# Filling four fifths instead of 0.55 of TensorE's planned gaps, in a kernel of windowed attention and a two-layer network

## The chip, the cores and the metric

The kernel runs on one core of one Trainium2 chip. The metric is the device time of one execution in microseconds (us), and where several executions were timed their median is given. The core has a matrix engine (TensorE, "PE" in the profile, with its weight loads on a row "PEld" of their own), a vector engine (VectorE, "DVE"), a scalar engine (ScalarE, "ACT"), GpSimd ("POOL"), a queue engine that issues transfers (SyncE, "SP"), and 16 DMA engines.

## What is computed

Eight batches of eight heads, 576 positions, 64 numbers per head. Each position attends to its neighbours within 32 positions and to 8 global positions, and the global positions attend to all. The result, 4608 tokens of 512 numbers, goes through a two-layer network with a softplus between the layers.

```python
mask = np.abs(pos[:, None] - pos[None, :]) <= window      # window = 32
mask = mask | is_global[:, None] | is_global[None, :]
scores = np.where(mask, scale * q @ k.T, -1e9)
attn = softmax(scores); y = attn @ v                      # (8, 8, 576, 64)
x = y.transpose(0, 2, 1, 3).reshape(4608, 512)
out = softplus(x @ w_in) @ w_out                          # w_in 512 x 2048, w_out 2048 x 512
```

## The kernel before, in words

The work is cut into jobs, and each job is a short run of instructions on one engine. Per batch, q and k are loaded, rounded to bf16 and transposed. For the first two batches TensorE does the transposes (tile `tr`, lines 857 to 863); later ones are transposed by VectorE. Blocks of 32 positions are taken four at a time ("pairs", 36 in all). A pair's scores are made on TensorE (tile `s`, line 1077), go through subtraction of the maximum, exponential and normalisation on VectorE, ScalarE and GpSimd (tiles `m`, `st`, `rs`, `pn`), and are transposed on VectorE (`pt`). For the first four pairs the mask is added on TensorE by a product with the identity (lines 1060 and 1070), and the exponential is a row of small ScalarE instructions (line 1113). The rows and columns of the global positions have tiles of their own (`sg`, `pg`, `pgt`, `ov`, `vg`). Four pairs make a stage of 512 tokens: TensorE multiplies probabilities by values (`xo`, line 1251), the result is rounded (`xT`), and then come the first layer (`h`, line 1286, 128 x 512 results of four matmuls each), softplus on ScalarE (`g`, line 1292), the second layer (`o`, line 1297) and the copy and store of the output (`osb`). There are nine stages. The attention of the next stage is interleaved with the two layers of the present one.

The order is not left to the hardware. Class `_Order` is a planner that runs when the program is built. Every job has an estimated cost, dependencies, and the PSUM banks that it opens. A fixed list, `ORDER`, says which job is taken next and on which engine; the planner walks through the list, gives each job a planned time (in planned nanoseconds), chooses PSUM banks by which of the eight was planned to come free first, and then writes the instructions out in order of planned time. It also keeps an estimate of instruction fetch: `stall()` (line 45) counts TensorE's instructions in blocks of 256 (`BLOCK`), with a first need at instruction 448 (`NEED`) and a first request at 130 (`ASK`), and moves planned times where a block would be late. `self.issued` is that count.

Where the planner takes a job for TensorE, it calls `keep()` (line 155) with the planned end of TensorE's last job, t0, and the planned start of the next, t1. If the gap is at least 700 planned ns, lies before 34,000 planned ns (`WARM`, line 358), and a PSUM bank is free, `keep()` puts fillers into it. A filler is a 128 x 128 by 128 x 512 product of zeros into that bank whose result nobody reads (`fill_in`, line 725; tile `warm`, line 729 of the profile), two instructions each: a weight load and a matmul. Their number is the gap times a share over a planned 220 ns (line 166). With `NARROW` at 0 only `FILL` and `FILLT` of line 151 are in use. The fillers stand in TensorE's own queue, so a job behind them starts when they are done, even if its data came earlier. `keep()` then books the bank as used until the planned end of the fillers and adds two per filler to `self.issued`; it does not move `free["PE"]`.

In the kernel before, the planner meets seven such gaps, of 7750.8, 1012.8, 1072.8, 2053.0, 815.2, 2020.9 and 820.6 planned ns, and puts 19, 2, 2, 5, 2, 5 and 2 fillers into them.

Of the kernel before, what the change touches and what calls it, by code (L numbers as in the profile page):

```python
# [20 lines left out]
class _Order:  # L21
# [126 lines left out]
        return self.backs[x - 1][1] if x else 0  # L148

    WARM = 0  # L150
    FILL, FILLT, NARROW, NFILL, NFILLT = 0.55, 220, 0, 0.8, 140
    STARVE = 900
    fill = None

# [1320 lines left out]
```

## Time and profile before

| What | us |
|---|---|
| Median of three runs | 335.49 |
| Lowest and highest of them | 334.19, 336.04 |
| The profiled execution's own time | 333.06 |
| Its span, first to last instruction | 331.4 |
| TensorE busy within the span | 317.9 |
| ScalarE, VectorE, GpSimd busy | 231.7, 220.9, 193.3 |

The profile is of one execution. The span leaves out 1.66 us that lie around it in that execution's own time. A matmul's recorded duration contains the run through the array, so matmuls that follow each other overlap in the record; how often one starts is read from the starts, not from the durations. "Idle before, releaser" names what ended an engine's wait; "issue" there means that the engine waited for nothing that the profile shows.

### The profile page before, as it was taken

What the parts mean: (1) busy time and instruction counts of PE and PEld (TensorE: products, weight loads), DVE (VectorE), ACT (ScalarE), POOL (GpSimd) and SP (SyncE); (2) the same over time, 40 slices, a digit from 0 to 9 for tenths busy, and PEclk for the clock granted to TensorE, in tenths of its full rate; (3) what the DMA queues carried; (4) which work ended last, traced back from release to release, by engine and by line L of the source; (5) the groups of instructions that cost most, each with busy time, mean ns of one, the idle gap of its engine ahead of it and who ended that gap; (6) DMA issues with size and microseconds to landing.
All of it is one profiled execution on the core that took longest, in us unless ns stands there. A gap on an engine that the chain in (4) does not pass through costs nothing.

```text
span 331.4 us, 12080 instructions
## 1 busy us (share of the span) xinstructions
PE 317.9 (96%) x5281; PEld 168.8 (51%) x5281; DVE 220.9 (67%) x387; ACT 231.7 (70%) x460; POOL 193.3 (58%) x173
## 2 busy tenths in 40 slices
PE   8778998899999999999999999999999999999995
PEld 3537874576555444544454445445544454454453
DVE  7697578786995999993895498819966890440000
ACT  5799759696897678489778947866457467925712
POOL 7865654994783596878648675496327764420000
PEclk9999999999999999999999999999999999999999
DMA  7999899898878998996994759650001112000102
GB/s 192 185 201 223 166 201 177 139 184 187 154 122 156 169 209 157 203 227 112 157 188 75 179 135 143 150 168 3 4 0 65 36 65 95 2 34 32 65 16 112
DMA packets 168860, 42.14 MB, mean 127 GB/s; under 512 B 153320, under 2 KB 165864, under 8 KB 168808
## 3 DMA queue, kind: packets, MB, share of 16 engines
q1 hardware_dynamic: 155928, 27.15, 46.0%
q0 software_dynamic: 11008, 11.08, 17.0%
q10 hardware_dynamic: 1872, 3.15, 2.5%
q8 instruction: 41, 0.67, 0.9%
q14 instruction: 11, 0.09, 0.1%
HBM read 36.71 MB, written 9.44 MB: 139 GB/s over the span
## 4 chain that ended last, share of the span: by engine, by line
PE 71%; SPq 11%; DMA 9%; ACT 4%; issue 1%; POOL 1%; DVE 1%; POOLq 0%
PE o L1297 32%; PE h L1286 29%; SPq L464 5%; PE xo L1251 4%; DMA stage<-in_q_dram 4%; SPq L469 3%; PE s L1077 3%; DMA stage<-in_k_dram 3%; ACT st L1113 2%; DMA wout<-in_moe_w_out_dram 2%; PE ov L997 1%; DMA stage<-in_v_dram 1%; SPq L518 1%; PE pick L886 1%; SPq L514 1%
## 5 line engine op out<-in xcount | busy, mean ns | idle before, releaser
L1297 PE MATMUL o<-wout,g 128*128 128x512 bf16 (+1 forms) x592 | 138.6, 374 | 0.2 <-ACT g L1292 0.2
L1286 PE MATMUL h<-xT,win 128*128 128x512 bf16 (+3 forms) x768 | 136.7, 326 | 0.8 <-DMA win<-in_moe_w_in_dram 0.8
L1292 ACT ACTIVATE g<-h 128x512 bf16<-128x512 f32 (+3 forms) x192 | 83.9, 503 | 35.0 <-PE h L1286 33.4
L1286 PEld LDWEIGHTS <-win 128*128 128x128 bf16 x768 | 66.7, 98 | 59.7 <-issue 1.1
L1132 POOL TENSOR_TENSOR pn<-st,rs 128x1024 bf16<-128x1024 f32 (+1 forms) x36 | 64.7, 1806 | 42.9 <-DVE rs L1126 38.8
L1297 PEld LDWEIGHTS <-g 128*128 128x128 bf16 x592 | 55.5, 98 | 60.6 <-ACT g L1292 1.4
L1100 POOL TENSOR_TENSOR st<-st,m 128x1024 f32<-128x1024 f32 x32 | 60.5, 1899 | 28.3 <-DVE m L1094 28.2
L1124 DVE TENSOR_REDUCE sm<-st 128x8 f32<-128x1024 f32 x32 | 38.4, 1200 | 19.0 <-ACT st L1117 18.8
L1081 DVE TENSOR_TENSOR st<-s,mask 128x512 f32<-128x512 f32 x64 | 41.3, 678 | 9.3 <-PE s L1077 9.2
L1094 DVE TENSOR_REDUCE m<-st 128x8 f32<-128x1024 f32 x32 | 38.4, 1206 | 0.4
L1117 ACT ACTIVATE st<-st 128x1024 f32<-128x1024 f32 x32 | 32.7, 1051 | 3.2 <-POOL st L1100 3.0
L1141 DVE STREAM_TRANSPOSE pt<-pn 128x512 int32<-128x512 int32 x36 | 24.6, 693 | 10.4 <-POOL pn L1132 10.2
L720 ACT COPY osb<-o 128x512 f32<-128x512 f32 (+1 forms) x27 | 15.5, 575 | 20.3 <-PE o L1297 18.7
L720 ACT CAST xT<-xo 128x512 bf16<-128x512 f32 (+3 forms) x28 | 11.5, 474 | 14.5 <-PE xo L1251 14.5
L720 POOL CAST kb<-stage 128x1152 bf16<-128x1152 f32 (+2 forms) x9 | 11.5, 1273 | 10.8 <-DMA stage<-in_q_dram 8.8
L717 POOL TENSOR_SCALAR qb<-stage 128x1152 bf16<-128x1152 f32 (+1 forms) x11 | 12.9, 1177 | 8.1 <-DMA stage<-in_q_dram 6.5
L1292 ACT ACT_TABLE_LOAD x13 | 16.7, 1283 | 0.2
L1077 PE MATMUL s<-kx,qx 64*32 64x128 bf16 x1152 | 14.7, 220 | 1.3 <-issue 0.6
L720 DVE CAST xT<-xo 128x512 bf16<-128x512 f32 (+3 forms) x20 | 11.0, 582 | 6.5 <-PE xo L1251 6.5
L1077 PEld LDWEIGHTS <-qx 64*32 64x32 bf16 x1152 | 10.0, 90 | 10.3 <-issue 7.7
L720 POOL CAST vb<-stage 128x1152 bf16<-128x1152 f32 x9 | 10.3, 1150 | 6.8 <-DVE sm L1124 3.3
L1117 ACT ACT_TABLE_LOAD x11 | 14.1, 1283 | 0.2
(129 smaller groups left out, 301.6 us busy)
## 6 DMA issues: line engine op xcount, KB each, us to landing
stage<-in_v_dram SPq DMA_DIRECT2D x56, 144.0 KB, 4.2
stage<-in_k_dram SPq DMA_DIRECT2D x48, 144.0 KB, 4.1
stage<-in_q_dram SPq DMA_DIRECT2D x48, 144.0 KB, 3.5
out_dram<-osb POOLq DMA_DIRECT2D x24, 256.0 KB, 3.6
out_dram<-osb ACTq DMA_DIRECT2D x11, 256.0 KB, 2.0
stage<-in_q_dram SPq DMA_DIRECT2D x4, 512.0 KB, 6.5
stage<-in_k_dram SPq DMA_DIRECT2D x4, 512.0 KB, 7.4
wout<-in_moe_w_out_dram POOLq DMA_DIRECT2D x4, 512.0 KB, 7.8
```

Source lines behind the costliest of these rows:

```text
L720: {"ACT": nc.scalar.copy, "DVE": V.tensor_copy, "POOL": nc.gpsimd.tensor_copy}[e](out, in_)
L1077: nc.tensor.matmul(out=PS["s", n, g][quad(a), x, :], lhsT=qx[b % 2][rows(g), a, j * BL:(j + 1) * BL], rhs=kx[b % 2][rows(g), a, e0 * BL:(e ...
L1081: V.tensor_tensor(out=PS["st", n][:, h, :, :], in0=PS["s", n, h][:, :, :], in1=mask[:, h, j0:j0 + PB, :, :].rearrange("p j s i -> p j (s i ...
L1094: V.reduce_max(out=m[:], in_=flat(PS["st", n], h0, h1), axis=AX)
L1100: on(e).tensor_tensor(out=t, in0=t, in1=over(PS["m", n, y][:], SL * BL), op=OP.subtract)
L1117: nc.scalar.activation(out=t, in_=t, func=AF.Exp)
L1124: V.reduce_sum(out=sm[:], in_=flat(PS["st", n], h0, h1), axis=AX)
L1132: on(e).tensor_tensor(out=PS["pn", n][:, :, :, h0:h1].rearrange("p x s h -> p h x s"), in0=PS["st", n][:, h0:h1], in1=PS["rs", n, y][:].re ...
L1141: V.transpose(out=bass.AP(base.tensor, base.offset, ap=[list(base.ap[0]), [2 * STEP, PB // 2], [STEP + BL // 2, 2], [1, SL * BL]]), in_=PS ...
L1286: nc.tensor.matmul(out=h[:, :], lhsT=w_in_t[c // 4][:, kd, c % 4 * P:(c % 4 + 1) * P], rhs=PS["xT", m][:, kd, lo:hi], start=(kd == 0), sto ...
L1292: nc.scalar.activation(out=PS["g", m, c][:, lo:hi], in_=PS[key][:, lo_of(c, hi - lo)], func=AF.Softplus)
L1297: nc.tensor.matmul(out=PS["o", m, ns, a][:, :], lhsT=PS["g", m, kf][:, ns * P:(ns + 1) * P], rhs=w_out_t[kf // 4][:, kf % 4, a:z], start=( ...
```

## The change

One constant is raised, the share of each planned gap that is filled. The list `ORDER`, the lower limit of 700 planned ns, the planned 220 ns per filler and everything else are the same text.

```diff
     WARM = 0
-    FILL, FILLT, NARROW, NFILL, NFILLT = 0.55, 220, 0, 0.8, 140
+    FILL, FILLT, NARROW, NFILL, NFILLT = 0.8, 220, 0, 0.8, 140
     STARVE = 900
     fill = None
```

The line that uses it is `count = int((t1 - t0) * share / step)`, with `share, step` being `FILL, FILLT`.

## The prediction

> **What bounds the kernel now.** I read the page first, then who TensorE waited for, then the fillers, then TensorE's instructions in order of time, and last a count of its instructions.
>
> ```profile
> PE 317.9 (96%) x5281; PEld 168.8 (51%) x5281; DVE 220.9 (67%) x387; ACT 231.7 (70%) x460; POOL 193.3 (58%) x173
> PE   8778998899999999999999999999999999999995
> q8 instruction: 41, 0.67, 0.9%
> ```
>
> TensorE is busy for 96% of the span, and its only slices below nine tenths, but for the last, are the first eight or so: up to about 70 us it waits for others, after that it is the bound. An us that its queue loses after 70 us is an us at the end; one lost before can be swallowed by a later wait. The third line is a queue that brings 41 pieces of about 16 KB under the kind "instruction"; it matters below. Whom TensorE waited for (total, times, longest):
>
> ```profile
> PE sg L968 <- issue: 1.0, 1, 1.0
> ...
> PE h L1286 <- DMA win<-in_moe_w_in_dram: 0.8, 1, 0.8
> ...
> PE s L1077 <- issue: 0.6, 1, 0.6
> PE xo L1251 <- ACT osb L720: 0.4, 1, 0.4
> ...
> PE xo L1251 <- ACT g L1292: 0.4, 1, 0.4
> PE xo L1251 <- DVE pt L1141: 0.2, 1, 0.2
> PE s L1077 <- ACT kx L720: 0.2, 1, 0.2
> PE o L1297 <- ACT g L1292: 0.2, 1, 0.2
> ```
>
> Behind 70 us only the last row remains, 0.2 us: there is next to no slack to hide a loss in. Two waits, 0.6 and 1.0 us, are for "issue", for nothing that the profile shows.
>
> **How many fillers come.** The fillers of before, and where they stand:
>
> ```profile
> L729 PE MATMUL warm<-vb x37: 376/379/634, 1.3 to 26.4; 128*128 128x512 bf16 x37
> ```
> ```profile
> 1.26 6.67 PE L729 MATMUL warm<-vb 128*128 128x512 bf16 x19 [1.26 <-DVE vb L551]
> 8.01 0.40 PE L857 MATMUL tr<-ident,kb 128*128 128x128 bf16 x4
> ...
> 10.57 0.40 PE L857 MATMUL tr<-ident,kb 128*128 128x128 bf16 x4 [0.66 <-ACT kb L720]
> ...
> 15.11 0.31 PE L860 MATMUL tr<-ident,qb 64*64 64x64 bf16 x8 [0.89 <-DVE m L1092]
> ...
> 16.46 1.24 PE L729 MATMUL warm<-vb 128*128 128x512 bf16 x5
> 19.19 0.43 PE L968 MATMUL sg<-kx,qg 128*32 128x320 bf16 x8 [1.49 <-DVE qg L720]
> ```
>
> Groups of 2 stand ahead of the rows of 10.57 and 15.11, and three more, of 2, 5 and 2, follow up to 26.4 us, 37 in all. A gap with n fillers is 400n to 400(n+1) planned ns long (220 / 0.55 = 400), and now gets one per 275 (220 / 0.8). By the groups alone 19 become 27 to 29, each 2 becomes 2 to 4, each 5 becomes 7 or 8: 12 to 24 more in all. By the planner's gaps of the kernel before it is 28, 3, 3, 7, 2, 7, 2, that is 52, or 15 more. I take 15, and 30 more instructions, since each filler is a weight load and a matmul.
>
> **What they cost where they stand.** Five fillers take 1.24 us of which the last is 0.376, so one starts every (1.24 - 0.376) / 4 = 0.216 us. The first group grows by 9, 1.94 us. Its last filler frees the array at 1.26 + 6.67 - 0.16 = 7.77 (the 0.16 is 0.376 less 0.216), the transpose starts at 8.01, so 0.24 was spare and the first transposes come 1.7 us later. The second and third group add 0.22 each: 2.1 us of delay, against TensorE's waits of 0.66, 0.2 (`s` for `kx`) and 0.89 up to 15.11. Some 0.4 us is left if what ends those waits doesn't move. ScalarE must not move much for that:
>
> ```profile
> 9.38 1.14 ACT L720 CAST kb<-stage 128x512 bf16<-128x512 f32 x2 [0.90 <-DMA stage<-in_k_dram]
> 14.64 0.42 ACT L713 ACTIVATE qb<-stage 128x256 bf16<-128x256 f32 x1 [0.93 <-DMA stage<-in_q_dram]
> ```
>
> It waits there for transfers that TensorE has no part in, so a late copy of a transpose has 0.93 us of cover before 14.64. The fourth group's two more (0.43) lie in the 1.49 us before `sg`; the sixth's two (0.43) lie ahead of the 0.8 us before `h`. If these covers were gone, the whole 1.94 + 0.22 + 0.22 + 0.43 + 0.43 = 3.2 us would be the cost; what passes 28 us by this sum is 0 to 0.4, and the 1.0 us of waits of `xo` at 64 to 69 us (0.4, 0.4, 0.2 in the waits) can take it. I cost the fillers' time at nothing, with 1.1 us as the far end. A gain is excluded as far as the clock goes: PEclk is at nine tenths or more in every slice, and its longest wait behind the first filler is the 1.49 us before `sg`.
>
> **What they move.** Every instruction behind 26.4 us now stands 30 places later in TensorE's queue. TensorE's instructions before two times, matmuls and weight loads:
>
> ```profile
> 0.00:46.60 46.60, 39.59 (x860) 26.44 (x861) 35.26 (x92) 37.55 (x136) 30.52 (x62) 1.00 1.19 193
> 0.00:52.00 52.00, 44.24 (x988) 29.79 (x989) 39.61 (x98) 40.05 (x148) 34.59 (x65) 1.00 1.19 193
> ...
> 0.00:72.20 72.20, 62.53 (x1356) 40.60 (x1357) 55.83 (x127) 56.78 (x180) 51.22 (x76) 1.00 1.14 184
> ...
> 0.00:172.90 172.90, 163.03 (x3274) 92.79 (x3275) 139.57 (x259) 134.01 (x307) 120.09 (x123) 1.00 1.01 177
> ...
> 0.00:234.49 234.49, 224.62 (x4137) 122.52 (x4137) 182.02 (x330) 177.95 (x372) 161.80 (x153) 1.00 0.89 161
> 0.00:236.10 236.10, 226.23 (x4298) 124.04 (x4299) 183.56 (x332) 178.54 (x373) 162.29 (x154) 1.00 0.88 160
> 0.00:239.10 239.10, 229.23 (x4311) 125.41 (x4312) 186.53 (x336) 181.11 (x377) 163.70 (x154) 1.00 0.87 158
> ```
> ```profile
> 46.33 0.25 PE L1077 MATMUL s<-kx,qx 64*32 64x128 bf16 x8
> 47.16 0.68 PE L1077 MATMUL s<-kx,qx 64*32 64x128 bf16 x56 [0.58 <-issue]
> ...
> 52.81 0.43 PE L968 MATMUL sg<-kx,qg 128*32 128x320 bf16 x8 [1.00 <-issue]
> ```
>
> The first two stretches end inside the two "issue" waits, and the counts are 860 + 861 = 1721 and 988 + 989 = 1977: exactly 256 apart. So the queue is fed in blocks of 256, and TensorE stood at the end of a block until the next was there. The transfers view has one "instruction" transfer in each of these stretches (in order: 44.8 to 45.85, 49.9 to 51.5, 71.1 to 72.6, 170.7 to 172, 236.5 to 237.5 us):
>
> ```profile
> q8 instruction: 1, 0.02, 5.6%
> q8 instruction: 1, 0.02, 5.7%
> q8 instruction: 1, 0.02, 5.8%
> q8 instruction: 1, 0.02, 5.9%
> q8 instruction: 1, 0.02, 6.0%
> ```
>
> The first two landed some 1.35 us before TensorE went on at 47.16 and 52.81; I take that for the others. [...] Whether a block comes in time hangs on where the multiple of 256 falls, and 30 instructions move it.
>
> I went through the block ends one by one: the end 30 instructions earlier, the request as much earlier, the landing as long after the request as before. Three come up short after 70 us.
>
> ```profile
> 66.71 0.83 PE L1286 MATMUL h<-xT,win 128*128 128x128 bf16 x12
> 67.38 0.81 PE L1297 MATMUL o<-wout,g 128*128 128x512 bf16 x3
> 68.03 0.83 PE L1286 MATMUL h<-xT,win 128*128 128x128 bf16 x12
> ...
> 236.09 1.90 PE L1297 MATMUL o<-wout,g 128*128 128x512 bf16 x8
> ```
>
> The largest: 1721 + 27 x 256 = 8633, less some 8 semaphore instructions of TensorE that the counts leave out, lies at 239.1 us (4311 + 4312 = 8623). Its block landed at 237.5 and was usable at 238.85, in time by 0.3. With the end 30 earlier, near 8595, it falls at 236.1 (8597), right behind `xo`. The request, 318 ahead, moves only within `xo` (behind the row of 234.49, 8274), by 0.2 us. Short by 238.85 - 0.2 - 236.1 = 2.55 us. The end four blocks behind the first (1721 + 1024 = 2745, near 74 us) moves to 72.2 (2713); its block landed at 72.6, and the request moves by 15 matmuls of the rows from 66.71 on, about 1.3 us: 72.6 + 1.35 - 1.3 - 72.2 = 0.45. The end 19 blocks behind the first (6585) moves to 172.9 (6549); landing 172, request 0.1 earlier: 0.3. In all **3.3 us**, behind 70 us, with nothing to hide them. If the transfer at 236.5 left at its request, near 234.6 and so 1.9 us sooner, 1.4 would be left; with 24 more fillers the same working gives 4.3.
>
> Before 70 us the block end at 46.6 moves 15 matmuls up, ahead of the eight `s` of the row and into small `h`, some 0.6 us, so that wait of 0.6 becomes 1.2; the one of 1.0 loses 0.2. These 0.4 go into the same 1.0 us before `xo` as the fillers' 0.4, and I cost them at nothing.
>
> The sum: 333.06 + 3.3 = 336.4 for an execution like the profiled one. The median of the runs is 2.43 above the profiled execution, so the forecast of a median is 335.49 + 3.3 = **338.8**.
>
> **The rivals.** First, no late block: the request may leave when the sequencer reads an instruction, ahead of the array, and then a block asked for in `xo` is asked for sooner than I reckon. For it: 41 blocks were drawn in, and only two show an "issue" wait now. Against it: those two waits are there, at 256 apart. Then the fillers alone count, 0 to 0.4: 335.5 to 335.9. [...]
>
> Second, the other side, faster: the block ends at 46.6 and 52.0 move off their short stretches and their waits go, 1.6 us, and the work behind them moves up with them. 333.9. It decides if the request of a block leaves in `o` and `h`, where 15 matmuls are 3.2 us earlier, and the transfer starts as much earlier. [...]
>
> Third, the fillers cost as well: ScalarE, busy from 15 to 30 us, takes over the 1.7 us and hands it down to `pn` and `xo` at 69 us. With the blocks, 335.49 + 3.3 + 1.7 = 340.5. Against it are the two ScalarE rows.
>
> **How the numbers follow.** A measurement of this kernel tells some 0.5%, 1.7 us, from no change. Forecast 0.59, first rival 0.27, second 0.05, third 0.09. Forecast and third rival are slower by over 0.5%: 0.68. The first is within: 0.27. The second lies at the bound of faster: 0.05. The range takes in the first rival's time and the forecast's own range: 335.3 to 340.3. The forecast's own range is 336.9 (1.4) to 340.2 (4.3 and the early delay of 0.4).
>
> **What would show it.** 52 `warm` matmuls, 28 of them in the first group, and `tr` from 9.7 us; waits of "issue" on TensorE at an `o` right behind `xo`, near 236 us, of about 2.5 us, and of about 0.4 near 72 and 173; the end of each of them a multiple of 256 instructions from the others; TensorE's busy time longer by 3.2 us of fillers. No "issue" wait after 70 us would prove the block working wrong, and a later `xo` than 69.3 us plus its lost slack would prove the cover of the fillers wrong.

## The result, and the profile after

The kernel after takes 337.55 us (median of 20 executions, 335.38 to 340.73), the kernel before 334.23 (20, 332.20 to 337.02). The ratio is 1.0093, with a 95% interval of 1.0067 to 1.0118: slower, by 3.1 us of 334.23 (2.2 to 3.9). Ratios, here and below, compare undisturbed executions only, those within 1.5% of the fastest of their kernel; medians are over all. The profiled execution of the kernel after took 339.67 us, 2.1 above its own median, while that of the kernel before (333.06) lies 1.2 below its median. So the two traces differ by more than the kernels do, and two more traces of the kernel after and one more of before, below, say which of the differences come back.

The page of the kernel after, the lines that answer to those of before:

```profile
PE 323.4 (96%) x5294; PEld 171.9 (51%) x5294; DVE 224.9 (67%) x387; ACT 231.7 (69%) x460; POOL 192.9 (57%) x173
PE   8959988998999999999999999999899999999995
PEclk9996997999999999999999999999999999999999
q8 instruction: 41, 0.67, 0.9%
```

There are 13 more matmuls and 13 more weight loads, not 15 of each. The clock line has two dips, in the fourth and the seventh slice, which the kernel before has not, and the 29th slice, 237 to 245 us, is no longer at nine tenths. Whom TensorE waits for, in the kernel after (total, times, longest):

```profile
PE h L1286 <- issue: 3.1, 2, 2.2
PE ov L997 <- issue: 1.6, 1, 1.6
PE ov L997 <- DVE pgt L987: 1.4, 1, 1.4
...
PE sg L968 <- DVE qg L720: 1.1, 1, 1.1
PE o L1297 <- issue: 1.0, 1, 1.0
PE tr L860 <- ACT qb L713: 0.6, 1, 0.6
```

The waits for "issue" are now 6 us where they were 1.6. The waits of `xo` at 64 to 69 us, 1.0 us in before, are gone: they were used up. TensorE's instructions in order of time, the fillers and the "issue" waits of the kernel after:

```profile
1.26 7.70 PE L729 MATMUL warm<-vb 128*128 128x512 bf16 x28 [1.26 <-DVE vb L551]
...
16.27 1.67 PE L729 MATMUL warm<-vb 128*128 128x512 bf16 x7
...
22.62 1.22 PE L997 MATMUL ov<-vb,pgt 32*32 32x129 bf16 x70 [1.42 <-DVE pgt L987]
25.41 0.28 PE L997 MATMUL ov<-vb,pgt 32*32 32x129 bf16 x2 [1.57 <-issue]
...
26.83 2.74 PE L729 MATMUL warm<-vb 128*128 128x512 bf16 x6
29.36 3.69 PE L1286 MATMUL h<-xT,win 128*128 128x128 bf16 x44
32.89 0.81 PE L729 MATMUL warm<-vb 128*128 128x512 bf16 x3
...
52.09 0.59 PE L1286 MATMUL h<-xT,win 128*128 128x128 bf16 x4 [2.22 <-issue]
...
73.54 0.38 PE L1251 MATMUL xo<-pt,vg 32*64 32x384 bf16 x8
78.05 1.14 PE L1286 MATMUL h<-xT,win 128*128 128x384 bf16 x6 [0.91 <-issue]
...
239.95 0.38 PE L1251 MATMUL xo<-pt,vg 32*64 32x384 bf16 x8
241.54 0.82 PE L1297 MATMUL o<-wout,g 128*128 128x512 bf16 x3
243.35 1.25 PE L1297 MATMUL o<-wout,g 128*128 128x512 bf16 x5 [0.99 <-issue]
```

The groups are 28, 3, 3 and 7, as forecast, but then 6 ahead of `h` and 3 within it: 50 in all. The groups of before at 20.43 and 23.97 us are not there. The planner counts its fillers' instructions in its own estimate of instruction fetch, and so the larger first groups moved its planned times; the gaps of 815, 2021 and 821 planned ns vanished, and others of 1663.8 and 903.9 came.

The counts of the kernel after's TensorE instructions up to four of its "issue" waits (windows from the start to inside the wait):

```profile
0.00:45.00 45.00, 38.35 (x732) 25.33 (x733) 31.29 (x87) 33.81 (x123) 28.52 (x61) 0.92 1.17 193
0.00:51.00 51.00, 43.15 (x860) 29.02 (x861) 35.58 (x92) 37.76 (x136) 30.69 (x63) 0.93 1.19 195
0.00:77.60 77.60, 68.21 (x1371) 44.11 (x1372) 57.47 (x128) 57.77 (x183) 52.44 (x76) 0.93 1.12 185
0.00:243.00 243.00, 232.33 (x4313) 127.44 (x4313) 189.00 (x335) 179.88 (x376) 163.30 (x154) 0.98 0.87 156
```

The sums are 1465, 1721, 2743 and 8626: 256 apart, then 4 x 256 less 2, then 23 x 256 less 5, the few missing being instructions that the counts leave out. 1721 is the very count at which the kernel before waited at 46.60 us; it lies at other work now.

Where the same instruction starts in both traces (after minus before, us):

| instruction, time in before | after | second trace (e0) | third trace (e10) | before again (e9) |
|---|---|---|---|---|
| first `h`, 27.63 | +1.73 | +2.54 | +1.97 | +0.15 |
| `xo`, 69.31 | +4.23 | +2.87 | +1.09 | -0.70 |
| `s`, 88.00 | +5.46 | +3.78 | +1.48 | -0.70 |
| `s`, 241.37 | +6.62 | +4.92 | +2.88 | -0.70 |

In each trace of the kernel after some of the loss stands there by 69 us, 1.1 to 4.2 us, and some comes behind it, 1.8 to 2.4.

### The profile page after: what moved, and what is told of

The parts are those of the page before. It is cut to its first block, busy times and chain, and to the rows that moved or that the text cites. A ratio compares the mean times of both kernels' runs of the same rounds, so it can differ in the third digit from the quotient of the medians.

```text
span 338.0 us, 12105 instructions
## 1 busy us (share of the span) xinstructions
PE 323.4 (96%) x5294; PEld 171.9 (51%) x5294; DVE 224.9 (67%) x387; ACT 231.7 (69%) x460; POOL 192.9 (57%) x173
## 4 chain that ended last, share of the span: by engine, by line
PE 67%; SPq 14%; DVE 7%; DMA 4%; issue 3%; ACT 3%; POOL 0%; DVEq 0%; ACTq 0%
PE o L1297 28%; PE h L1286 28%; SPq L464 9%; PE xo L1251 4%; SPq L469 3%; DMA stage<-in_q_dram 3%; PE s L1077 2%; PE ov L997 2%; DVE st L1081 1%; DVE m L1094 1%; SPq L518 1%; DMA stage<-in_v_dram 1%; DVE sm L1124 1%; PE warm L729 1%; SPq L514 1%
## 5 line engine op out<-in xcount | busy, mean ns | idle before, releaser
L1286 PE MATMUL h<-xT,win 128*128 128x512 bf16 (+3 forms) x768 | 139.0, 330 | 3.1 <-issue 3.1
L1286 PEld LDWEIGHTS <-win 128*128 128x128 bf16 x768 | 68.5, 100 | 63.1 <-issue 4.5
L729 PE MATMUL warm<-vb 128*128 128x512 bf16 x50 | 14.5, 445 | 1.3 <-DVE vb L551 1.3
```

The lines of the kernel that those rows point to most:

```text
L1286: nc.tensor.matmul(out=h[:, :], lhsT=w_in_t[c // 4][:, kd, c % 4 * P:(c % 4 + 1) * P], rhs=PS["xT", m][:, kd, lo:hi], start=(kd == 0), sto ...
```

## The experiments

Two theories stood against each other. **Blocks:** the added instructions move the ends of the 256-instruction blocks, and blocks that come late behind 70 us are the loss. **Fillers:** the fillers' own time, or what it does to the first 70 us, is the loss. Some expectations name a third, the **plan** theory: that the banks and the planned times that the planner chose anew are the loss. The **early** theory there puts the loss into the first 60 us alone, and the **clock** theory into the half clock at 25 to 31 us. In most experiments the plan of fillers is written out: each group takes from a list how many full fillers (512 columns) and how many tiny ones (32 weight columns, 8 columns) it gets; groups behind the list's end keep their number.

```diff
-        ps = psum(key, [P, 512], FP32)
-        w = P if thin else 4 * P
-        for x in range(n):
-            nc.tensor.matmul(out=ps[:, 0:w], lhsT=idle[:, 0, :], rhs=idle[:, 0, :] if thin else idle, start=True, stop=True)
+        wide, narrow = PLAN.pop(0) if PLAN else (n, 0)
+        ps = psum(key, [P, 512], FP32) if wide + narrow else None
+        for x in range(wide + narrow):
+            nc.tensor.matmul(out=ps[:, :] if x < wide else ps[0:32, 0:8], lhsT=idle[:, 0, :] if x < wide else idle[:, 0, 0:32], rhs=idle if x < wide else idle[:, 0, 0:8], start=True, stop=True)
```

**The kernel after again** (no edit).

> The changed kernel once more, for its spread. Blocks theory (late blocks of 256 instructions are the cost): waits of 'issue' on TensorE near 78 and 243 us again, about 0.9 and 1.0 us, since these follow from the count of instructions; ratio 1.006 to 1.012. Fillers theory (their time and place in the first 34 us, and the half clock that came with them, are the cost): the half-clock stretches at 25 to 31 and 52 to 55 us come again and the time from 76 us to the end is not longer than in the kernel before.

Median 337.86 us, ratio 1.0125 (1.0078 to 1.0171). The trace has the same "issue" waits: 2.20 at 26.2 us, 0.53 at 45.7, 1.67 at 52.1, 0.51 at 76.3 and this one:

```profile
241.65 1.25 PE L1297 MATMUL o<-wout,g 128*128 128x512 bf16 x5 [0.94 <-issue]
```

The places come back to the instruction; the lengths vary by up to 0.6 us. The late ones sum to 1.45 here, 1.9 in the first trace. The half clock at 25 us came again, that at 52 us did not (0.50 at 28 to 31 us and 1.00 at 52 to 55, where the first trace has 0.50 and 0.51), and between `xo` and 241 us this trace loses 2.05 us against before, which the fillers theory excluded.

**The kernel before, and 13 tiny products** at the end of the first group, so that 26 instructions are added and little time (the first transposes start 0.51 us later).

```diff
+    PLAN = [(19, 13)]
```

> The kernel before with its own fillers, and 13 more products of 8 columns (32 weight columns) at the end of the first group: the 26 more instructions of the changed kernel, nearly without their time, and with the plan and the banks of the kernel before. Blocks theory: the late waits of 'issue' near 74 to 78 us (0.4 to 0.9) and near 237 to 243 us (1.0 to 2.5) come as in the changed kernel, so over 1.4 us after 70 us, 0.5 to 1.0% slower in all. Fillers theory: no change within 0.2%, since the fillers' time grows by about 0.4 us, of which 0.24 is spare. Plan theory (other banks and planned times): no change either, since the plan is that of before.

Median 336.29, ratio 1.0075 (1.0043 to 1.0108). TensorE's order of time in this kernel:

```profile
73.80 2.64 PE L1286 MATMUL h<-xT,win 128*128 128x384 bf16 x31 [1.33 <-issue]
...
239.45 1.45 PE L1297 MATMUL o<-wout,g 128*128 128x512 bf16 x6 [1.48 <-issue]
```

At `xo` of 69.31 us this trace is 0.37 ahead of before; at 88 it is 1.13 behind and at 241 2.92 behind. Tiny products in the place of the added fillers give most of the loss, and nearly all of it in two late blocks, 2.81 of the 3.29 us between `xo` and 241: this is the blocks theory, and the fillers theory would have had no loss here, nor the plan theory, since the plan is that of before. Two early waits for blocks, 1.58 us at 25.41 and 1.40 at 47.93, left no delay at `xo`.

**The kernel before, and 144 instructions more.**

```diff
+    PLAN = [(13, 78)]
```

> The kernel before, its first group made of 13 full fillers and 78 products of 8 columns in place of 19 full ones: 144 more instructions in the queue, the group about as long. Blocks theory, from the block ends of the trace of before moved by 144: late blocks near 106, 145, 178 and 213 us, 1.5 to 2.4 us each, none near 243; 8 us in all (6 to 10), 2 to 3% slower, over twice what the change cost with far less filler time. Fillers theory: no change within 0.3%. Plan theory: no change.

Median 353.25, ratio 1.0436 (1.035 to 1.0523). The waits named for behind 70 us came, at the ends that now fall into the next stages' `xo`, and the one near 240 is gone:

```profile
110.98 0.17 PE L1251 MATMUL xo<-pt,vb 32*64 32x32 bf16 x1 [2.15 <-issue]
...
151.90 0.72 PE L1077 MATMUL s<-kx,qx 64*32 64x128 bf16 x35 [2.93 <-issue]
187.19 0.24 PE L1251 MATMUL xo<-pt,vb 32*64 32x64 bf16 x13 [3.16 <-issue]
...
224.67 0.21 PE L1251 MATMUL xo<-pt,vb 32*64 32x32 bf16 x5 [2.52 <-issue]
```

They sum to 10.8 where 8 was expected, with 15.8 lost between 69 and 241 us. The traced execution, 354.71 us, is one of the longer of the six (345.98 to 355.51). Some 1.5 of the rest came at 74 to 78 us of before, most of it a wait of 1.35 for VectorE's `pick`, and some is the clock, which with each of the two longest waits is at a half all through windows of 3.3 and 3.2 us (a window, its length, then busy us and instructions of TensorE, its weight loads, VectorE, ScalarE and GpSimd, then the granted clock, the DMA share and GB/s):

```profile
151.30:154.60 3.30, 2.37 (x39) 1.19 (x40) 1.91 (x4) 0.66 (x1) 0.08 (x1) 0.50 1.22 250
188.80:192.00 3.20, 3.20 (x9) 1.19 (x8) 3.20 (x5) 2.91 (x3) 0.00 (x0) 0.50 0.02 5
```

**The kernel after, moved on by a whole block** (256 instructions more than before, so that the ends lie at the same work as in before).

```diff
+    PLAN = [(10, 133)]
```

> The changed kernel with its plan, banks and later groups (3, 3, 7, 6, 3), its first group made of 10 full fillers and 133 products of 8 columns in place of 28 full ones: 256 more instructions than the kernel before, one whole block, so that every block ends at the work where it ended before. Blocks theory: no 'issue' wait after 70 us, and the time within 0.5% of the kernel before, the rest of the cost being what the first 34 us leave. Fillers theory and plan theory: as slow as the changed kernel, 0.6 to 1.2%.

Median 336.57, ratio 1.0072 (1.004 to 1.0104), between the two theories. The trace has no "issue" wait of 0.3 us or more behind 70 us, as the blocks theory says; but it is 1.11 us behind before already at the first transposes, 0.55 at `xo` and 1.06 at the end. The kernel with wider products, below, says something of why.

**The kernel after, cut to 37 fillers**, so that the instruction count is that of before, while the first four groups hold 37 in place of 28.

```diff
+    PLAN = [(28, 0), (3, 0), (3, 0), (3, 0), (0, 0), (0, 0)]
```

> The changed kernel's plan and banks, with only 37 fillers in its groups: 28, 3, 3, 3, 0, 0 for 28, 3, 3, 7, 6, 3. The count of instructions is that of the kernel before behind the groups, the first three groups are as long as in the changed kernel. Blocks theory: no 'issue' wait after 70 us, the wait at 25 us shorter than 1.6 us, time within 0.5% of the kernel before. Plan or first-groups theory: 0.6% slower or more, as the changed kernel.

Median 334.54, ratio 1.0025 (0.9993 to 1.0058). No late wait; near 236 us the trace reads as before's:

```profile
236.05 1.90 PE L1297 MATMUL o<-wout,g 128*128 128x512 bf16 x8
```

It is 1.64 us late at the first transposes, 0.13 at the first `h` and 0.04 ahead at `xo`: the larger first group is swallowed by the waits behind it, and this is the plan of the kernel after, so that the plan theory falls too. One of the twelve executions took 531.32 us, which nothing here explains; the others took 332.50 to 335.68. ScalarE, the same instruction as in the prediction's second row of it:

```profile
14.65 0.42 ACT L713 ACTIVATE qb<-stage 128x256 bf16<-128x256 f32 x1 [0.31 <-DMA stage<-in_q_dram]
```

It starts 0.01 us later than in before, its wait 0.93 reduced to 0.31.

**The kernel after, a whole block on, with wider small products** (143 of 100 columns, `0:100` in place of `0:8` in the line above, so that TensorE is not idle at the start).

```diff
+    PLAN = [(0, 143)]
```

> As the run with one whole block more, but the first group is 143 products of 100 columns (with 32 weight columns) and no tiny ones, so that the array streams all through the group; again 256 more instructions than the kernel before, with the changed kernel's plan, banks and later groups. Blocks theory: no 'issue' wait after 70 us; if it was the array's idling in the tiny products that held the run with tiny ones back (half clock near 10 us), the clock stays whole there and the time is within 0.4% of the kernel before. If it is 0.6% slower or more with neither, the cost lies in the later groups or the plan, against the blocks theory.

Median 335.59, ratio 1.0061 (1.0025 to 1.0097): again no late wait, and again about a us late from the start (1.10 at the first transposes, 0.71 at `xo`, 1.23 at the end), with the clock whole (1.00 up to 243 us). ScalarE and, from the transfers of 8.4 to 9.75 us, the instruction queue of this kernel:

```profile
15.80 0.42 ACT L713 ACTIVATE qb<-stage 128x256 bf16<-128x256 f32 x1 [1.84 <-DMA stage<-in_q_dram]
```
```profile
q8 instruction: 1, 0.02, 6.0%
```

The last load of q lands 1.2 us later than in before. Here and in the two kernels above with 133 and 78 tiny products (15.94 and 15.95 us in place of 15.80) a block of instructions is fetched while q and k are loaded, and in before and with 37 fillers none is before 14 us. The test so seems to have added a cost of its own, and these two kernels show only that the late waits go when the ends lie where they lay; whether all of their 2.0 to 2.4 us is that load isn't settled.

**The kernel before, 3 fillers less** (6 instructions less).

```diff
+    PLAN = [(16, 0)]
```

> The kernel before with 16 fillers in its first group for 19: 6 fewer instructions. Blocks theory, from the block ends moved by 6 the other way: no late wait, the waits at 47 and 52 us from 1.6 us together to 0.6 or less, time equal to 0.3% faster (they go mostly into the waits of xo at 64 to 69 us). Fillers theory: the half clock of the start lasts as long, the first transposes come at 8.0 us as before, no change.

Median 334.48, ratio 1.0032 (0.9998 to 1.0067). No late wait, but two early ones that were not expected:

```profile
31.94 0.65 PE L1251 MATMUL xo<-pt,vb 32*64 32x96 bf16 x58 [1.20 <-issue]
...
45.16 0.61 PE L1077 MATMUL s<-kx,qx 64*32 64x128 bf16 x26 [1.86 <-issue]
```

At `xo` and behind it this trace is 1.5 to 1.8 us late, where it was expected no later than before. A miss: before 70 us, where the other queues are loaded (a mean DMA share of 1.19 up to 51 us and of 0.87 up to 243 in this trace), the counts alone don't say how long a block takes.

**The kernel that the prediction described**, 52 fillers as 28, 3, 3, 7, 2, 7, 2 in the order of before.

```diff
+    PLAN = [(28, 0), (3, 0), (3, 0), (7, 0), (2, 0), (7, 0), (2, 0)]
```

> The plan of the kernel before with the groups that the prediction gave the changed kernel: 28, 3, 3, 7, 2, 7, 2, where the planner in fact gave 28, 3, 3, 7, 0, 0, 6, 3. 30 more instructions than before, and the fillers at 20 and 24 us stay. Blocks theory: waits of 'issue' near 72 to 76 us (0.4 to 1.5) and 236 to 243 us (1.0 to 2.6) and at 47 us (1.2 or more); 0.6 to 1.2% slower. Clock theory (what made the changed kernel slower is the half clock at 25 to 31 us, after the fillers of 20 and 24 us went): the clock stays whole there, and the time is within 0.4% of the kernel before.

> A second profile of the 28, 3, 3, 7, 2, 7, 2 fillers on the plan of before, whose first profile was the fastest of its six executions (334.99 against a median of 337.86): the wait near 238 us again (1.5 to 2.2), and what the slower executions add, by the early-stage theory a wait of 'issue' at 25 us long enough for half clock behind it, over 2 us of lag left at 70 us.

Median 337.86, ratio 1.0123 (1.0067 to 1.0178). The two traces (334.99 and 334.81 us) have one late wait:

```profile
238.04 1.89 PE L1297 MATMUL o<-wout,g 128*128 128x512 bf16 x8 [1.94 <-issue]
```

and 2.08 in the other, at the place named. At `xo` they stand 0.29 and 0.03 us ahead of before: in these two the fillers' time is swallowed, as costed. But the other five executions of the first took 337.0 to 340.6, and what those had more isn't in a trace.

**13 tiny products late**, at about 75 us, so that nothing ahead of it changes.

```diff
-                PS["o", m, ns, a] = psum(("o", m, ns, a), [P, z - a], FP32)
+                PS["o", m, ns, a] = psum(("o", m, ns, a), [P, z - a], FP32); [nc.tensor.matmul(out=PS["o", m, ns, a][0:32, 0:8], lhsT=idle[:, 0, 0:32], rhs=idle[:, 0, 0:8], start=True, stop=True) for x in range(13 if (m, ns) == (1, 0) else 0)]
```

> The kernel before, untouched up to 76 us; there 13 products of 8 columns (32 weight columns) are put ahead of one of the second layer's first matmuls, into the bank that this matmul then clears. 26 more instructions from there on, 0.4 us of their own. Blocks theory: one wait of 'issue' of 1.0 to 2.0 us near 237 us, which the kernel before doesn't have, perhaps 0.1 to 0.3 near 173, none at 74 to 78: 1.4 to 2.7 us slower in all, 0.4 to 0.8%. Early theory (the cost of the change arises in the first 60 us alone): 0.4 us slower, 0.1%, no wait near 237 us.

Median 335.07, ratio 1.0043 (1.0007 to 1.0078). One "issue" wait of over 0.2 us behind 70 us:

```profile
238.47 1.46 PE L1297 MATMUL o<-wout,g 128*128 128x512 bf16 x6 [1.32 <-issue]
```

The trace is 0.09 us ahead of before at `xo`, 0.43 behind at 88 us, past the products themselves, and 1.94 behind at 241: 1.5 for a wait of 1.32. 1.0043 is 1.4 us of 333.4 (0.2 to 2.6): the late wait is paid for in full, with an untouched early part.

**The kernels before and after, one more trace each, on the same chip.**

> A second profile of the kernel before, for how far its own waits differ from one execution to the next: block ends at the same counts, waits of 'issue' near 47 and 52 us of 0.3 to 2 us each, none over 0.3 after 70 us; the clock whole until the end, or half for one stretch of 3.4 us before 60 us.

> A third profile of the changed kernel: half clock from about 25 us for 6.8 us as in the two before it, waits of 'issue' at 26 us (over 1 us), 52, 76 to 78 (0.4 to 1) and 241 to 244 us (0.9 to 1.1).

332.37 and 335.83 us. Of the 3.46 between them 1.8 is there by `xo`, about 0.4 comes at 74 to 88, and the rest is the late wait:

```profile
239.61 1.25 PE L1297 MATMUL o<-wout,g 128*128 128x512 bf16 x5 [1.11 <-issue]
```

The other waits of the kernel after came at their places, but shorter than expected: 0.72 us at 25.65, 0.85 at 50.36, and nothing of 0.2 us or more near 74. The kernel before has 0.21 and 0.73 at its two places, and a stretch at half clock that its first trace has not, 3.41 us from 15.50.

The granted clock is what the three traces of the kernel after share in the first 70 us. The window from 28 to 31 us in before, in after, in its second and its third trace, and in the kernel with the forecast's 52 fillers, in this order (columns as above, the clock third from the end):

```profile
28.00:31.00 3.00, 3.00 (x105) 2.82 (x103) 2.81 (x5) 2.97 (x12) 1.04 (x1) 1.00 1.09 302
```
```profile
28.00:31.00 3.00, 3.00 (x20) 2.09 (x19) 2.86 (x5) 2.90 (x11) 1.04 (x1) 0.50 0.99 284
```
```profile
28.00:31.00 3.00, 3.00 (x14) 1.58 (x13) 2.49 (x8) 2.98 (x16) 1.21 (x2) 0.50 1.10 294
```
```profile
28.00:31.00 3.00, 3.00 (x24) 1.90 (x23) 2.86 (x6) 2.98 (x12) 1.10 (x2) 0.61 0.97 253
```
```profile
28.00:31.00 3.00, 2.88 (x49) 2.60 (x48) 2.86 (x8) 2.98 (x12) 1.04 (x1) 1.00 0.97 274
```

The clock is a half for 6.83 us in each of the three, from 24.77, 24.76 and 23.53 us, and whole there in every trace of the forecast's kernel, of before, and of the one with 37 fillers (1.00 at 28 to 31 us). A half clock as such need not cost: the second trace of before and the one with 37 fillers have 3.41 us of it, from 15.50 and 19.69, and are 0.70 and 0.04 us ahead of before at `xo`. In the kernel after TensorE had little to do just ahead of it:

```profile
21.00:25.40 4.40, 1.42 (x102) 1.07 (x78) 3.73 (x12) 4.17 (x20) 2.12 (x3) 0.93 1.08 178
```

It is busy for 1.42 of these 4.40 us: it waits 1.42 us for `pgt` and 1.57 for a block, and the fillers that stood at 20.43 and 23.97 are gone. In before it was busy for 3.40 of them, and `h` came when its weights did:

```profile
21.00:25.40 4.40, 3.40 (x115) 2.01 (x113) 4.16 (x14) 4.32 (x23) 1.98 (x4) 1.00 1.12 185
```
```profile
27.63 2.56 PE L1286 MATMUL h<-xT,win 128*128 128x128 bf16 x43 [0.81 <-DMA win<-in_moe_w_in_dram]
```

At half clock the six fillers from 26.83 take 2.74 us, where the same six take 1.47 in the kernel with 133 tiny products, and `h` starts at 29.36. Then 44 of its small matmuls take 3.69 us where 43 took 2.56. The wait for `pgt` that had ended ahead of the fall was of 1.42, 1.42 and 1.68 us in the three traces. In the first trace the clock fell 0.9 us into the second of the two waits, and in the third right behind the first wait and ahead of the one for the block. That row, and those of two kernels in which the clock stayed whole, the second trace of the forecast's kernel and the kernel of 143 wider products:

```profile
23.11 1.82 PE L997 MATMUL ov<-vb,pgt 32*32 32x129 bf16 x70 [1.68 <-DVE pgt L987]
```
```profile
25.70 0.24 PE L997 MATMUL ov<-vb,pgt 32*32 32x129 bf16 x4 [1.58 <-issue]
```
```profile
23.87 1.23 PE L997 MATMUL ov<-vb,pgt 32*32 32x129 bf16 x72 [1.67 <-DVE pgt L987]
```

With the fillers of 20 us in place and those of 24 us right behind it, at 25.87, a wait of 1.58 for the block left the clock whole (1.00 at 21 to 25.4 us); without either but with no block end there, so did a wait of 1.67 for `pgt` (1.00). How little work is too little isn't shown.

## Why the prediction was right, and where it was not

The sign, the size (3.3 us against a measured 3.1) and one of the mechanisms held, but only about half of the size came from where the prediction put it; two errors, a late part sized too large and an early part costed at nothing, offset each other, so that the close agreement is in part luck. It is the difference that compares: the forecast of 338.8 stood on 335.49 for the kernel before, which over 20 executions is 334.23.

**The number of fillers** was taken as 15 more "by the planner's gaps of the kernel before". That step failed. The gaps are not the kernel before's: a filler's two instructions enter the planner's fetch estimate, and it came to 13 more, from the fifth group on in other places.

**"I cost the fillers' time at nothing, with 1.1 us as the far end."** For the fillers as assumed this held in the traces: 0.04 us ahead of before at `xo` with 28, 3, 3, 3, and 0.03 to 0.29 ahead with all 52. The 0.93 us of ScalarE's wait was the cover, and it sufficed. The 1.94 us by which the first group was to grow were 1.03, 1.02 and 2.10 in the three traces of the kernel after (28 fillers in 7.70, 7.69 and 8.77 us), so the first transposes came at 8.80, 8.79 and 9.86. For the fillers as they came the step failed: the kernel after is 1.1 to 4.2 us late at `xo`. What the three traces share is the half clock over `h` (0.50, 0.50 and 0.61 at 28 to 31 us) behind the emptied 21 to 25 us. What differs are the waits for blocks ahead of 70 us: 4.15, 4.40 and 1.77 us, where before has 1.58; the third trace, with hardly more of them than before, is still 1.1 late. In the first a second stretch at half clock, of 3.41 us from 52.08, comes with the wait of 2.22 at 52 us. No run changes the clock alone, so that the half clock is the cause is argued, not shown. The two traces of the kernel with 52 fillers, which has both groups, 20 and 24 us in before, have a whole clock at 28 to 31 us (1.00); that the groups don't decide alone is what the kernels with 133 and 143 small products show, which have neither and a whole clock there too (1.00). "A gain is excluded as far as the clock goes" was right, but a loss was not looked for, as the clock of before showed none.

**The late blocks** are the step that the experiments bear out best: 13 tiny products bring them, 37 fillers take them away, 144 instructions move them to the four named stages, and 13 products at 75 us bring the last alone. Their sizes were off in both directions, and the sum was 1.9, 1.45 and 1.1 us in the three traces of the kernel after instead of 3.3:
- The term of 2.55 at 236 us measured 0.94 to 1.11. Three matmuls of `o`, 0.65 us, stand between `xo` and the end, two of them since 26 instructions came and not 30. And the transfer, which the prediction let move by 0.2 us, moved by 1.0:

```profile
q8 instruction: 1, 0.02, 5.5%
```

This row is of the stretch 240.9 to 242.1 us of the kernel after: the transfer begins 1.0 us after `xo` (239.95), while in before it began 2.0 after it (234.49 to 236.5). 2.55 less 0.65 less 0.8 gives 1.1. No run shows how far ahead of its end a block is asked for: the 318 instructions of that working, and so the 0.2 us of the request, were an assumption, and the same holds for the requests in the other two terms. What the traces show is when a transfer begins: in before 52, 82 and some 24 instructions ahead of the end, at 44.88, 49.97 and 236.54 us (1669 of 1721, 1895 of 1977 and 8601 of some 8625), in the kernel after 100 ahead, at 241.00 (8526 of 8626). The prediction's other case, a transfer that leaves at its request, 1.9 us sooner, would have left 0.65 here (1.4 in all three terms) and, less the two matmuls, 0.2; the truth lay between the two.
- The term of 0.45 at 72 us measured 0.91 and 0.51 (at 78.05 and 76.30), and under 0.2 in the third trace.
- The term of 0.3 at 173 us is not there.

With the forecast's 52 fillers the first of these was 1.94 and 2.08, still under 2.55, and the other two were not there.

**The early blocks**, costed at nothing ("that wait of 0.6 becomes 1.2"), came at other work and, in two traces of three, longer: 1.57 and 2.22 us in the first, 2.20 and 1.67 in the second, 0.72 and 0.85 in the third. They are hard to place, as the kernel with 3 fillers less showed.

**The rivals.** "No late block" fell: the late blocks cost 0.5 to 3.2 us each here. What spoke for it holds all the same for most of the 41 blocks, two of which show a wait in before and five in after; but it said nothing of an end right behind `xo`. The faster case did not come. The third, ScalarE handing on 1.7 us, was right that the first 70 us would cost, and wrong in the way: ScalarE had 0.31 us left in the kernel with the same first three groups and 37 fillers.

**What stays open.** How the 3.1 us of the median divide: 1.8 to 2.4 is lost behind 69 us in the three traces, 1.1 to 1.9 of it in late waits, which leaves 0.7 to 1.3 of the median for the early part, where the traces have 1.1 to 4.2. Why the transfer begins 1.0 us after `xo` in the kernel after and 2.0 in before. And the untraced executions of the kernel with 52 fillers: its ratio of 1.0123 is 4.1 us, where its two traces show one late wait of some 2.

No version here beats the kernel before; those with 37 fillers in the groups of after and with three fillers less can't be told from it.

## What to carry to other kernels

Here 26 added instructions that delayed the first transposes by 0.51 us moved the later ends of the blocks of 256 and brought two late waits, of 1.33 and 1.48 us: count the instructions that are added, however short they are, and see which ends come to lie in or right behind a stretch of small, quick matmuls (161 in 1.61 us in the `xo` from 234.49 us of before), where the next block came too late here. Where a planner counts what it inserts, its gaps after a change are not those before it, so rebuild its plan in thought with the inserted work, and see which inserts go: in the kernel after those of 20 and 24 us went, and its clock at 28 to 31 us was 0.50 to 0.61 where before has 1.00, though that the one made the other isn't shown. And where executions of one kernel differ by 2 us, one trace of each tells the places, not the shares.

## What was not expected of the hardware

- In the three kernels in which a block of instructions, some 16 KB (0.67 MB in 41 transfers), is fetched between 8 and 12 us, while q and k are loaded, the last load of q lands 1.2 to 1.3 us later (ScalarE goes on at 15.80 to 15.95 in place of 14.64).
- The clock fell to a half behind a single wait of 1.68 us (third trace of the kernel after), and stayed so for 6.83 us; waits of 1.59 and 1.67 left it whole in the two kernels a block on (1.00 at 21 to 25.4 us).
- With the late blocks of 2.9 and 3.2 us the clock was at a half (0.50 all through 151.30 to 154.60 and 188.80 to 192.00 us). Of the 15.8 us that this kernel lost between 69 and 241 us, the four late waits are 10.8 and the delay at 74 to 78 us some 1.5; that the half clock made the rest isn't shown.
